# Another order of the steps of an attention and two-layer network kernel on one Trainium2 core

## The chip, the core and the metric

The kernel runs on one core of a Trainium2 chip. The metric is the time of one execution on the device in microseconds (us); shorter is better. A core has a matrix engine (TensorE, PE in the profile), a vector engine (VectorE, DVE), a scalar engine for functions like exp (ScalarE, ACT), a general engine (GpSimd, POOL), and SyncE (SP), which here issues DMA transfers. Each engine runs its own queue of instructions in order and waits at an instruction until what it needs is there. Operands lie in SBUF (the large on-chip memory); TensorE writes its sums to PSUM, a small memory of banks from which the other engines read them.

## The reference

Two stages. The first is attention with root-mean-square normalised q and k, for 8 batches and 12 heads of 448 rows of 64 values; the second takes the heads of a row as 768 features, multiplies by `w_in` (768 x 2048), applies a leaky rectifier with a slope per feature, and multiplies by `w_out` (2048 x 768).

```python
rms = np.sqrt(np.mean(x * x, axis=-1, keepdims=True) + 1e-06)   # for q and for k
q_n, k_n = q / rms_q * g_q, k / rms_k * g_k
scores = 1.0 / np.sqrt(64) * np.matmul(q_n, k_n.transpose(0, 1, 3, 2))
attn = np.exp(scores - np.max(scores, axis=-1, keepdims=True))
attn = attn / (np.sum(attn, axis=-1, keepdims=True) + 1e-09)
x = np.matmul(attn, v)                      # to 3584 rows of 768
h = x @ w_in
g = np.maximum(h, 0.0) + alpha * np.minimum(h, 0.0)
out = g @ w_out                             # 3584 x 768, float32
```

## The kernel before

**Steps.** The kernel is a set of small functions, one for each kind of step, and a string `PLAN` (lines 24 to 195) with 1324 calls of them. At its end a loop goes through `PLAN.split()` and calls one function for each word. The order of the words is the order in which every engine gets its instructions. Nothing reorders them afterwards; waits between engines follow from the data, and from the buffers that are used again. So the string is the schedule, written out by hand or by a program that made it.

**Attention.** The work is cut into 24 units y (three to a batch, four heads each) and seven slices j of 64 queries. For each unit:
- `load_qk(y)` (SP) brings q and k into tiles called `nat`, of which there are four, so q and k of two units (units 2, 5 and 8 use a lent piece of SBUF, `arena`). From unit 9 on it is `load_twice`, eight transfers on SP (L326). `load_v(b)` (GpSimd's queue, L334) brings v of a batch; there is one buffer for it, so the load waits for the attend steps of the batch before.
- `square` (GpSimd; L370 from unit 9 on, L381 before), `reduce` (VectorE, L391 or L400) and `root` (ScalarE, L421 and L422) make the norms; `scale` multiplies by them (GpSimd, L428 from unit 9 on, L441 before; for the first units VectorE). `fold`, `weigh`, and `turn` (TensorE transposes, L565) or `flip` (VectorE, L536) bring q and k into the layout for the products. Unit 0 does this in pieces, `part_square`, `part_reduce`, `part_root`, `part_scale` (L479), `part_turn`, `part_copy`.
- `score(y,j)` (TensorE, L593), `soft(y,j)` (ScalarE's exp, L607), `den` and `attend` (TensorE, L618 and L642: sums of the exponentials and their product with v), `log`/`invert` (ScalarE), and `times` (VectorE, L714), which writes `xT`.

**The two layers.** For each batch b, `up(b,ft)` (TensorE, L731, six matmuls; the first four of batch 0 start with `begin`) multiplies by a block of 128 of the 2048 columns, `slope` (ScalarE, L771) and `larger` (VectorE, L777) make the rectifier and write `gT`. Row tiles 0 to 5 go through `down` (TensorE, L797, 16 matmuls), `down_end` (VectorE, L808) and a send (SP, L783). Tiles 6 to 27 go in pairs by a scheme that saves matmuls in return for sums: `mix_weights` (GpSimd, L827) sums blocks of `w_out` once; for each pair, `mix_two(tile, engine)` and `mix_rest(tile)` sum blocks of `gT`, and the products are `qa1`, `qa2`, `qa3`, `qb1`, `qb2`, `qc1`, `qc2` (TensorE, L859) with steps `...v` of VectorE that add them up and send them. The last three pairs use `quad`.

The sums of a pair are these; `eng` is VectorE for the pairs 6 to 20 (`vec`) and GpSimd for the others (`pool`), and `mix_rest` is GpSimd's and reads `s2`:

```python
        eng.tensor_add(out=s1, in0=block(tile + 1, 0), in1=block(tile + 1, 1))   # L847
        eng.tensor_sub(out=s2, in0=s1, in1=block(tile, 0))                       # L848
```

**Buffers.** PSUM is split into three pools: two double banks for scores (`pss`), one double bank for den and attend (`psa`) and two single banks for the rest (`psf`). Steps take the buffers of a pool in turn. The last argument of score, up, den, attend, down, begin and the products, `spare`, sends a step to another pool than its own. Results on their way out lie in five buffers (`osb`, from `result()`); one is free again when its send is through. The weights are loaded in pieces on GpSimd's queue, `load_w_in(c)` (four or eight issues, L344 and L352) and `load_w_out(c)` (L358). `spin` is a matmul without a use, which keeps TensorE at work in the opening; `follow` is a small copy that holds GpSimd's queue to a place.

Of the kernel before, what the change touches and what calls it, by code (L numbers as in the profile page):

```python
# [24 lines left out]
opening() part_square(q,0:1,0:7,act) part_square(q,1:2,0:7,act) part_reduce(q,0:1,0:7)  # L25
part_reduce(q,1:2,0:7) part_root(q,0:7) load_v(0) load_w_in(1) part_square(k,0:2,0:3,act)
# [3 lines left out]
part_copy(q,0:7,vec) part_turn(k,r3-7) part_copy(k,0:3,vec) square(2,q) reduce(1,k) follow(0,k)  # L30
part_copy(k,3:7,vec) score(0,0,0) square(2,k) reduce(2,q,0) soft(0,0) score(0,1,0) root(1) spin(1)
scale(1,q) score(0,2,1) load_w_in(0) soft(0,2) square(3,q) scale(1,k) score(0,4,0) soft(0,1)
square(3,k) reduce(2,q,1) follow(1,k) score(0,3,1) turn_one(1,q) soft(0,4) score(0,6,0)
turn_one(1,k) reduce(2,k) spin(1) score(1,0,1) soft(0,3) score(1,2,0) soft(0,6) soft(1,0)
spin(2,0) spin(1) score(1,1,1) score(0,5,0) soft(1,2) root(2) spin(1) soft(1,1) score(1,6,0)
scale(2,q) soft(0,5) score(1,3,1) scale(2,k) load_w_in(2) reduce(3,q,None) load_qk(4) soft(1,3)
score(1,5,0) turn(2) score(1,4,1) soft(1,5) score(2,0,0) soft(1,6) soft(1,4) soft(2,0)
score(2,1,0) reduce(3,k,0+1) den(0+1,0) soft(2,1) attend(0+1,1,0) root(3) scale(3,q) log(0+1)
load_qk(5) score(2,3,1) score(2,4,0) invert(0+1) soft(2,4) attend(0+1,0,1) soft(2,3) score(2,2,0)
times(0+1,1,0) times(0+1,1,1) square(4,q) load_qk(6) spin(1,0) times(0+1,0,0) score(2,5,1)  # L40
scale(3,k) turn(3) reduce(4,q,None) load_w_in(3) load_qk(7) square(4,k) soft(2,2) score(2,6,0)
soft(2,5) soft(2,6) den(2,1) attend(2,0,1) score(3,0,1) score(3,1,0) square(5,q) log(2)
reduce(4,k,None) invert(2) root(4) begin(0) begin(1) times(2,0,0) up(0,0,0) begin(2) square(5,k)
up(0,1,0) begin(3) soft(3,0) slope(0,0) reduce(5,q) up(0,2,0) load_w_out(0) slope(0,1) larger(0,0)
reduce(5,k) square(6,k) up(0,3,1) up(0,4,0) soft(3,1) score(3,6,0) score(3,2,0) slope(0,4)
soft(3,2) larger(0,1) up(0,5,0) slope(0,2) up(0,6,0) scale(4,q) root(5) slope(0,3) soft(3,6)
square(6,q) larger(0,3) scale(4,k) score(3,3,0) larger(0,4) larger(0,2) load_w_out(1) scale(5,q)
square(7,q) reduce(6,q) load_v(1) slope(0,5) larger(0,5) follow(2,k) slope(0,6) score(3,5,0)
soft(3,5) turn(4) up(0,8,0) score(3,4,1) score(4,0,0) soft(3,3) score(4,4,0) up(0,9,0) slope(0,8)
scale(5,k) soft(4,0) up(0,11,0) larger(0,6) up(0,7,1) larger(0,8) up(0,10,0) load_w_out(2)  # L50
up(0,12,0) score(4,2,1) soft(3,4) slope(0,9) reduce(6,k) slope(0,11) score(4,3,0) larger(0,9)
slope(0,7) score(4,1,0) soft(4,4) up(0,13,0) slope(0,10) larger(0,11) load_qk(8) larger(0,7)
larger(0,10) slope(0,12) soft(4,2) larger(0,12) soft(4,1) slope(0,13) turn(5) up(0,14,0)
larger(0,13) soft(4,3) score(5,0,1) square(8,k) score(5,2,0) square(8,q) root(6) slope(0,14)
reduce(7,q) up(0,15,0) score(4,5,0) soft(5,0) larger(0,14) scale(6,k) soft(4,5) score(4,6,1)
slope(0,15) larger(0,15) down(0,0,0) reduce(8,q) score(5,6,0) scale(6,q) soft(5,2) score(5,1,0)
score(5,4,1) reduce(8,k) soft(4,6) soft(5,6) down(1,0,0) turn(6) score(5,3,0) load_w_out(3)
soft(5,4) den(3+4,1) square(7,k) attend(3+4,0,0) soft(5,1) reduce(7,k) soft(5,3) down_end(0,0)
log(3+4) mix_weights(0,1) invert(3+4) down_end(1,0) load_qk(9) score(5,5,0) score(6,0,0)
attend(3+4,1,0) root(7) down(2,0,1) scale(7,q) soft(5,5) soft(6,0) times(3+4,0,0) den(5,1)  # L60
mix_weights(0,0) times(3+4,1,1) attend(5,0,1) score(6,3,0) mix_weights(0,2) root(8) load_qk(10)
score(6,1,1) log(5) invert(5) down_end(2,0) times(3+4,1,0) down(0,1,0) times(5,0,2) scale(7,k)
times(5,0,3) score(6,4,1) score(6,5,0) scale(8,k) score(6,2,0) soft(6,1) times(5,0,0) times(5,0,1)
soft(6,3) down_end(0,1) turn(7) square(9,q) mix_weights(0,3) up(1,2,1) square(9,k) soft(6,4)
slope(1,2) up(1,1,0) soft(6,2) reduce(9,q) down(1,1,0) scale(8,q) up(1,0,0) larger(1,2)
score(7,0,0) score(6,6,0) up(1,4,1) slope(1,1) up(1,3,0) larger(1,1) score(7,4,0) down_end(1,1)
soft(6,5) slope(1,0) larger(1,0) score(7,3,0) soft(6,6) soft(7,0) slope(1,4) up(1,7,0)
mix_weights(1,0) reduce(9,k) slope(1,3) square(10,q) soft(7,3) slope(1,7) larger(1,4) up(1,5,1)
larger(1,3) larger(1,7) soft(7,4) turn(8) score(7,5,0) slope(1,5) soft(7,5) score(7,1,0) soft(7,1)
up(1,6,0) slope(1,6) load_v(2) larger(1,5) up(1,10,0) score(7,2,0) root(9) slope(1,10)  # L70
score(8,3,0) score(7,6,1) load_qk(11) square(10,k) up(1,9,0) up(1,8,0) reduce(10,q) larger(1,6)
scale(9,q) larger(1,10) soft(7,6) soft(7,2) up(1,13,1) up(1,11,0) slope(1,9) slope(1,8)
slope(1,13) reduce(10,k) slope(1,11) larger(1,9) larger(1,8) fold(10) scale(9,k) mix_weights(3,0)
root(10) larger(1,13) larger(1,11) up(1,12,0) scale(10,q) mix_weights(1,2) slope(1,12)
square(11,q) den(6+7,0) flip(9,k) score(8,0,0) scale(10,k) log(6+7) soft(8,0) up(1,15,0)
slope(1,15) up(1,14,1) load_qk(12) soft(8,3) down(2,1,0) larger(1,12) square(11,k) slope(1,14)
square(12,q) flip(9,q) score(8,1,0) larger(1,14) score(8,2,1) larger(1,15) score(8,4,0)
invert(6+7) down(3,0,0) down_end(2,1) soft(8,2) score(8,6,0) soft(8,1) score(8,5,1) soft(8,4)
down_end(3,0) weigh(9) soft(8,5) soft(8,6) reduce(11,q) flip(10,k) attend(6+7,0,1) times(6+7,0,0)
attend(6+7,1,0) times(6+7,1,0) flip(10,q) score(9,0,0) down(3,1,1) weigh(10) reduce(11,k) fold(11)  # L80
score(9,2,0) score(9,1,0) down_end(3,1) times(6+7,1,1) down(4,0,0) soft(9,0) root(11) soft(9,2)
# [1021 lines left out]
```

## Time and profile before

| what | value |
|---|---|
| time, median of 3 executions | 426.65 us (425.70 to 428.54) |
| the profiled execution, its own time | 428.47 us |
| its span in the profile | 426.4 us |
| TensorE's mean granted clock | 0.979 of full speed |

The profile is of one execution. Its span runs from the first to the last instruction that is seen; the time holds some 2 us more around it. A line such as L847 is a line of the kernel above. A row of a group has the line, engine, operation, the tile written and the tiles read with their shape and type, the number of instructions, then the busy time, the mean length in ns of one, and the engine's idle time just before them with who ended it. A row of a timeline has the start, the length, engine, line, operation and tiles, the number of instructions run together, and in brackets the idle time before and who ended it. A row of a window has the time from and to, its length, the busy time and count of PE, PE's weight loads, DVE, ACT and POOL, the granted clock, the busy share of the DMA engines (as an average of 16; the records let it pass 1) and GB/s. "issue" is idle time in which the engine waited for nothing that the profile shows.

### The profile page before, as it was taken

Reading aid. Unit: us, or ns where it says so; the run is one execution under the profiler, and the core shown is the slowest. Engines: PE = TensorE matmul, PEld = TensorE weight load, DVE = VectorE, ACT = ScalarE, POOL = GpSimd, SP = SyncE. Lnnn points to the kernel's source line nnn. Section 1 sums busy time; section 2 is a strip of 40 time slices with the busy share of each in tenths; the row PEclk is TensorE's granted clock in tenths of the full one; section 3 lists DMA queues with packets and bytes.
Section 4 is the critical chain, followed back from the end, with each engine's and each line's share of the span. In section 5 each row is a group of like instructions: output and inputs, shape, how many; then the busy total and the mean of one; then the engine's idle time right before and its main releaser. Section 6 shows DMA issues by size and latency. Waiting matters only on the chain. (4 is left out here: it accounts for less than half of the span.)

```text
span 426.4 us, 11986 instructions
## 1 busy us (share of the span) xinstructions
PE 402.5 (94%) x5083; PEld 211.3 (50%) x5083; DVE 289.3 (68%) x495; ACT 269.6 (63%) x405; POOL 269.3 (63%) x184
## 2 busy tenths in 40 slices
PE   7689999799999999999998999969989999999996
PEld 3334444355455545454455445534545445555564
DVE  3868865456837878697787968996798565464422
ACT  5488686437876686666875896857666875225210
POOL 7899867975585988975475866385464234700780
PEclk9599999799999999999999999999999999999999
DMA  8999795997393875763975965792602600320133
GB/s 240 248 230 238 137 243 95 195 231 143 83 223 97 213 165 97 177 159 97 208 160 120 204 155 133 149 237 83 156 20 49 111 2 22 73 59 0 29 93 102
DMA packets 37221, 58.39 MB, mean 137 GB/s; under 512 B 4768, under 2 KB 28976, under 8 KB 37168
## 3 DMA queue, kind: packets, MB, share of 16 engines
q1 hardware_dynamic: 23232, 45.43, 43.0%
q0 software_dynamic: 13536, 11.81, 18.5%
q8 instruction: 39, 0.64, 0.6%
q10 hardware_dynamic: 400, 0.39, 0.3%
q14 instruction: 14, 0.11, 0.1%
HBM read 58.40 MB, written 11.01 MB: 163 GB/s over the span
## 5 line engine op out<-in xcount | busy, mean ns | idle before, releaser
L607 ACT ACTIVATE expT<-sc 128x896 f16<-128x896 f32 x168 | 147.5, 916 | 58.6 <-PE sc L593 54.1
L731 PE MATMUL hT<-xT,w_in_sb 128*128 128x448 f16 x558 | 116.4, 353 | 4.5 <-DVE gT L777 3.9
L731 PEld LDWEIGHTS <-w_in_sb 128*128 128x128 f16 x768 | 72.5, 98 | 79.0 <-issue 15.6
L428 POOL TENSOR_TENSOR qs<-nat,rr 128x896 f16<-128x896 f32 x30 | 65.3, 2231 | 46.9 <-ACT rr L422 46.9
L777 DVE TENSOR_TENSOR gT<-hT,gT 128x448 f16<-128x448 f32 x93 | 57.5, 621 | 35.4 <-ACT gT L771 34.8
L771 ACT ACTIVATE gT<-hT,cols 128x448 f16<-128x448 f32 x92 | 58.2, 635 | 35.1 <-PE hT L731 34.5
L370 POOL TENSOR_TENSOR nat<-nat 128x896 f32<-128x896 f32 x30 | 50.9, 1700 | 15.3 <-DMA nat<-in_q_dram 9.4
L593 PE MATMUL sc<-qT,kT 64*32 64x448 f16 (+1 forms) x1092 | 51.0, 360 | 5.4 <-ACT expT L607 1.9
L859 PEld LDWEIGHTS <-gT 128*128 128x128 f16 x352 | 33.9, 98 | 24.3 <-issue 2.1
L731 PE MATMUL hTa<-xT,w_in_sb 128*128 128x448 f16 x198 | 42.9, 353 | 0.0
L593 PEld LDWEIGHTS <-kT 64*32 64x32 f16 (+1 forms) x1092 | 16.3, 94 | 34.9 <-issue 25.9
L391 DVE TENSOR_REDUCE sp<-nat 128x28 f32<-128x896 f32 x30 | 32.1, 1076 | 0.1
L714 DVE TENSOR_TENSOR xT<-av,rden 64x448 f16<-64x448 f32 (+1 forms) x37 | 27.2, 735 | 6.6 <-ACT rden L676 4.6
L777 DVE TENSOR_TENSOR gT<-hTa,gT 128x448 f16<-128x448 f32 x33 | 20.4, 619 | 13.8 <-ACT gT L771 13.6
L771 ACT ACTIVATE gT<-hTa,cols 128x448 f16<-128x448 f32 x33 | 21.0, 636 | 11.0 <-PE hTa L731 10.9
L618 PEld LDWEIGHTS <-vt 64*32 64x32 f16 x1344 | 20.3, 93 | 14.8 <-issue 5.0
L797 PEld LDWEIGHTS <-gT 128*128 128x128 f16 x192 | 18.9, 102 | 16.1 <-issue 5.5
L797 PE MATMUL op<-w_out_sb,gT 128*128 128x384 f16 x144 | 24.8, 326 | 0.0
L618 PE MATMUL av<-expT,vt 64*32 64x448 f16 x896 | 24.4, 349 | 0.0
L855 POOL TENSOR_TENSOR gT<-gT 128x1024 f16<-128x1024 f16 x11 | 23.9, 2172 | 0.6 <-DVE arena L847 0.6
L847 POOL TENSOR_TENSOR gs<-gT 128x1024 f16<-128x1024 f16 x3 | 6.4, 2117 | 26.8 <-DVE gT L777 26.8
L859 PE MATMUL qx<-w_out_sb,gT 128*128 128x384 f16 x112 | 19.7, 326 | 0.0
(154 smaller groups left out, 570.0 us busy)
## 6 DMA issues: line engine op xcount, KB each, us to landing
nat<-in_q_dram SPq DMA_DIRECT2D x60, 216.0 KB, 4.6
nat<-in_k_dram SPq DMA_DIRECT2D x60, 216.0 KB, 5.9
out_dram<-osb SPq DMA_DIRECT2D x107, 96.0 KB, 3.0
vt<-in_v_dram POOLq DMA_DIRECT2D x8, 672.0 KB, 7.4
w_in_sb<-in_moe_w_in_dram POOLq DMA_DIRECT2D x24, 128.0 KB, 8.1
w_out_sb<-in_moe_w_out_dram POOLq DMA_DIRECT2D x4, 768.0 KB, 8.5
nat<-in_k_dram SPq DMA_DIRECT2D x6, 448.0 KB, 7.8
nat<-in_q_dram SPq DMA_DIRECT2D x5, 448.0 KB, 7.2
```

What stands on the lines that cost most here:

```text
L370: nc.gpsimd.tensor_mul(out=sqs[y, nm], in0=t[:, :, :HD], in1=t[:, :, :HD])
L391: nc.vector.tensor_reduce(out=parts[y][:, ts("qk".index(nm), 4 * J), :1], in_=sqs[y, nm], axis=AXIS_X, op=ALU.add,)
L428: nc.gpsimd.tensor_mul(out=t.rearrange("p j d n -> p n j d"), in0=nat[y, nm][:, :, :HD].rearrange("p (n j) d -> p n j d", j=J), in1=r.unsq ...
L593: nc.tensor.matmul(out=sc[ds(64 * g + m * c, m), par, :S].rearrange("p (j c) -> p j c", j=J), lhsT=kT[ds(64 * par, 64), j, g, ts(c, m)], r ...
L607: nc.scalar.activation(out=expT[y][:, j], in_=scs[y, j][:, :, :S], func=AF.Exp, scale=QK_SCALE, bias=EXP_BIAS,)
L618: nc.tensor.matmul(out=accs[g][ds(32 * n, 32), :S], lhsT=weights(g, y, par, c, j), rhs=expT[y][ds(64 * g, 64), j, par, :], start=(j == 0), ...
L714: nc.vector.tensor_mul(out=o, in0=p, in1=q)
L731: nc.tensor.matmul(out=hT[:, :S], lhsT=w_in_sb[:, block_of(g, i), ts(ft, 128)], rhs=xT[b][:, g, i, :], start=(i == 0 and g == 0), stop=(i ...
L771: nc.scalar.activation(out=g, in_=hT[:, :S], func=AF.Copy, scale=alpha_sb[:, ft : ft + 1])
L777: nc.vector.tensor_max(out=g, in0=hT[:, :S], in1=g)
L797: nc.tensor.matmul(out=op[:, :OH], lhsT=gT[:, ft, ts(tile % J, 128)], rhs=w_out_sb[:, ft, ts(oh, OH)], start=(ft == 0), stop=(ft == NF - 1),)
L859: nc.tensor.matmul(out=bank[:, c], lhsT=g[:, ft], rhs=v[:, ft, c], start=(first and ft == 0), stop=(ft == HF - 1), skip_group_check=True,)
```

## The change

Only the string `PLAN` is another one: 1324 steps before and after, of each kind as many, so each engine has the same instructions with the same shapes. What differs is the order of the words and the last argument (`spare`, the PSUM pool) of some hundred steps. The table is one line shorter, so lines behind it have numbers lower by one in the kernel after. No function is touched.

The diff takes out nearly all of the table's lines and puts in others. These are the places that the prediction speaks of. The opening, before and after:

```diff
-opening() part_square(q,0:1,0:7,act) part_square(q,1:2,0:7,act) part_reduce(q,0:1,0:7)
...
-load_qk(3) part_square(k,0:2,3:7,act) part_reduce(k,0:2,0:3) part_reduce(k,0:2,3:7)
-part_root(k,0:3) part_scale(q,0:7,7,pool) part_scale(k,0:3,3,vec) part_turn(q,r0-7) square(1,q)
-reduce(1,q) part_root(k,3:7) part_scale(k,3:7,4,vec) part_turn(k,r0-3) gains() square(1,k)
...
-part_copy(k,3:7,vec) score(0,0,0) square(2,k) reduce(2,q,0) soft(0,0) score(0,1,0) root(1) spin(1)
-scale(1,q) score(0,2,1) load_w_in(0) soft(0,2) square(3,q) scale(1,k) score(0,4,0) soft(0,1)
+opening() part_square(q,1:2,0:7,act) load_w_in(1) part_square(q,0:1,0:7,act)
+part_reduce(q,0:1,0:7) part_reduce(q,1:2,0:7) part_root(q,0:7) part_square(k,0:2,0:3,act)
+part_reduce(k,0:2,0:3) part_square(k,0:2,3:7,act) part_reduce(k,0:2,3:7) part_root(k,0:3)
+square(1,q) part_scale(k,0:3,3,vec) load_v(0) reduce(1,q) spin(2,0) part_turn(k,r0-3)
+part_scale(q,0:7,7,pool) load_qk(3) part_turn(q,r0-7) gains() part_copy(q,0:7,vec)
+part_copy(k,0:3,vec) part_root(k,3:7) square(1,k) score(0,0,0) reduce(1,k) part_scale(k,3:7,4,vec)
+soft(0,0) square(2,q) score(0,1,1) reduce(2,q,0) part_turn(k,r3-7) part_copy(k,3:7,vec)
+score(0,2,1) spin(1) root(1) load_w_in(0) scale(1,k) scale(1,q) soft(0,1) score(0,3,0)
+score(0,5,0) soft(0,3) turn_one(1,k) turn_one(1,q) square(2,k) spin(1,0) score(0,4,0) reduce(2,k)
...
+soft(1,6) load_w_in(2) scale(2,q) scale(2,k) spin(1) soft(1,3) root(3) turn(2) soft(1,5)
+scale(3,q) soft(0,6) score(1,4,0) soft(1,4) score(2,0,0) score(2,1,1) scale(3,k) soft(2,0)
```

Units 13 to 15 and the sends of the first tiles:

```diff
-square(12,k) down(5,1,0) times(8,0,0) load_qk(13) times(8,0,1) mix_weights(1,1) down(4,1,0)
...
-slope(2,5) up(2,9,1) larger(2,3) reduce(13,q) larger(2,4) slope(2,8) load_qk(14) soft(10,4)
...
-qa2v(6) scale(13,q) load_qk(15) score(11,4,0) slope(2,15) score(11,1,0) reduce(14,q) reduce(14,k)
...
-score(12,0,0) score(11,2,0) scale(13,k) down_end(5,0) mix_two(6,vec) times(9+10,0,0) root(14)
+score(8,2,1) load_qk(12) score(8,3,0) down_end(2,1) weigh(9) load_qk(13) soft(8,1) down(3,0,0)
+score(8,5,0) soft(8,2) score(8,4,1) attend(6+7,0,1) square(11,q) score(9,0,0) down_end(3,0)
...
+scale(10,k) square(11,k) score(9,1,0) reduce(11,k) soft(8,5) load_qk(14) fold(11) mix_weights(1,2)
+times(6+7,1,0) soft(8,4) down_end(3,1) down(4,0,0) square(12,q) soft(9,0) times(6+7,1,1)
+flip(10,k) down_end(4,0) soft(8,6) load_qk(15) mix_weights(3,3) soft(9,1) root(11) score(9,5,0)
...
+larger(2,15) score(12,3,0) mix_weights(2,2) soft(12,0) scale(13,k) larger(2,13) mix_two(6,vec)
+qa3(6,0) mix_rest(6) down_end(5,0) times(9+10,0,0) qb1(6,0) mix_weights(3,0) times(9+10,1,0)
```

The sums of the pairs 12, 14 and 16:

```diff
-up(4,3,1) scale(17,k) up(4,4,0) soft(15,6) mix_two(12,vec) up(4,0,0) score(16,1,0) soft(16,3)
...
-larger(4,14) score(18,1,0) load_qk(22) root(20) qb2v(12) load_v(6) den_pre(17) attend(17,0,1)
-score(18,5,0) soft(18,1) log_pre(17) flip(19,k) scale(20,k) invert(17) flip(19,q) times(17,0,1)
...
-up(5,1,0) up(5,3,1) up(5,2,0) soft(18,2) slope(5,0) up(5,5,0) mix_two(14,vec) up(5,7,1) up(5,4,0)
-score(19,6,0) slope(5,1) square(21,q) score(19,1,0) soft(19,0) up(5,8,0) larger(5,0) slope(5,3)
-larger(5,1) up(5,6,1) scale(20,q) square(21,k) qa1(14,0) slope(5,2) qa2(14,0) score(19,4,0)
...
-attend(18+19,0,1) root(22) mix_two(16,vec) score(20,4,1) times(18+19,0,0) attend(18+19,1,0)
+mix_two(12,vec) score(16,3,1) load_v(5) soft(16,3) soft(15,1) up(4,1,0) up(4,4,0) slope(4,1)
...
+soft(18,1) qb2v(12) den_pre(17) load_qk(22) scale(19,k) log_pre(17) attend(17,0,1) flip(19,k)
+scale(20,k) invert(17) score(18,3,0) flip(19,q) times(17,0,0) score(18,5,1) qc2(12,0)
+score(18,2,1) square(21,q) qc1(12,0) soft(18,5) times(17,0,1) qc2v(12) times(17,0,3) scale(20,q)
+soft(18,2) square(21,k) times(17,0,2) weigh(19) square(22,q) qc1v(12) up(5,0,0) score(19,1,0)
+score(18,4,1) score(19,0,0) up(5,1,0) soft(18,3) up(5,5,1) reduce(21,q) slope(5,0) mix_two(14,vec)
...
+slope(5,7) slope(5,8) load_v(6) slope(5,4) larger(5,2) up(5,6,1) soft(19,0) soft(19,1) larger(5,7)
...
+score(20,5,0) log(18+19) larger(5,15) flip(21,q) mix_two(16,vec) attend(18+19,0,1) score(20,1,1)
```

More of the change, by code (lines that the diff above doesn't have):

```diff
@@ L37 @@
[L37 to L48, printed above, removed]
@@ L55 @@
[L55 to L66, printed above, removed]
@@ new lines @@
+times(9+10,1,1) soft(12,3) fold(14) score(11,2,1) score(11,6,0) qa3v(6) qb1v(6) score(11,5,0)
+qb2(6,0) qc2(6,1) flip(13,k) soft(11,3) square(15,q) soft(11,2) root(14) qc1(6,0) qb2v(6) qc2v(6)
+qc1v(6) score(12,2,1) load_qk(16) scale(14,q) flip(13,q) score(12,1,0) reduce(15,q) soft(11,6)
+soft(11,5) weigh(13) score(12,6,0) den_pre(11) attend(11,0,0) soft(12,2) soft(12,1) mix_two(8,vec)
+soft(12,6) log_pre(11) score(13,0,0) score(13,3,0) invert(11) qa1(8,0) square(15,k) times(11,0,3)
+soft(13,0) qa1v(8) qa2(8,0) qa3(8,0) times(11,0,1) qb1(8,0) score(13,1,0) soft(13,3) qa2v(8)
@@ new lines @@
+slope(3,14) larger(3,14) square(17,k) score(14,6,0) soft(14,5) qa1(10,0) reduce(17,q) qc2(8,0)
+qa2(10,1) score(14,4,0) attend(12+13,0,1) reduce(17,k) soft(14,6) fold(17) soft(14,3) log(12+13)
+weigh(15) scale(16,q) invert(12+13) mix_two(10,vec) qa1v(10) attend(12+13,1,0) root(17) qc2v(8)
+soft(14,4) qa2v(10) score(15,0,0) times(12+13,0,0) times(12+13,1,0) soft(15,0) score(15,2,0)
+qa3(10,1) score(15,3,0) times(12+13,1,1) flip(16,k) flip(16,q) soft(15,2) weigh(16) den_pre(14)
+attend(14,0,1) score(15,4,0) soft(15,3) score(16,0,1) qa3v(10) mix_rest(10) load_qk(19)
```

260 lines of the change are left out of this document (131 added, 129 removed).

## The prediction

> **What bounds the kernel now.** The page comes first: its span and the busy time of each engine.
>
> ```profile
> span 426.4 us, 11986 instructions
> ...
> PE 402.5 (94%) x5083; PEld 211.3 (50%) x5083; DVE 289.3 (68%) x495; ACT 269.6 (63%) x405; POOL 269.3 (63%) x184
> ...
> L428 POOL TENSOR_TENSOR qs<-nat,rr 128x896 f16<-128x896 f32 x30 | 65.3, 2231 | 46.9 <-ACT rr L422 46.9
> ...
> L370 POOL TENSOR_TENSOR nat<-nat 128x896 f32<-128x896 f32 x30 | 50.9, 1700 | 15.3 <-DMA nat<-in_q_dram 9.4
> ```
>
> TensorE (PE) is busy for 402.5 of 426.4 us, and the other engines for about two thirds. The change alters no instruction, only the order and the pools of PSUM (the accumulator memory), so TensorE's work stays. It can win at most 426.4 − 402.5 = 23.9 us of TensorE idle, plus what a low TensorE clock costs; it can lose without a bound. The last two rows price one GpSimd scale (2.23 us) and one square (1.70 us). Next, the view of waits, for TensorE alone (sum, count, longest):
>
> ```profile
> PE hT L731 <- DVE gT L777: 3.9, 2, 3.2
> PE avb L618 <- issue: 2.7, 1, 2.7
> ...
> PE sc L593 <- ACT expT L607: 1.9, 3, 0.8
> ...
> PE sc L593 <- DVE xT L714: 1.4, 1, 1.4
> ...
> PE tps L565 <- POOL qs L441: 0.6, 2, 0.3
> ```
>
> Three waits, 3.9 in two pieces and 1.4, go to VectorE although VectorE has slack on average. The 2.7 is a pause for which no engine is to blame. Much of the rest stands before 41.3 us, in the opening. I take these three places in turn.
>
> **VectorE's sums.** The view of lines, shapes kept apart, has VectorE's additions and subtractions of two f16 SBUF operands (`mix_two(…,vec)`, one L847 and one L848 each):
>
> ```profile
> L847 DVE TENSOR_TENSOR arena<-gT 128x1024 f16<-128x1024 f16 x7 | 10.8, 1542 | 0.0
> L848 DVE TENSOR_TENSOR arena<-arena,gT 128x1024 f16<-128x1024 f16 x7 | 7.9, 1135 | 0.2
> L847 DVE TENSOR_TENSOR gs<-gT 128x1024 f16<-128x1024 f16 x1 | 0.7, 682 | 0.0
> L848 DVE TENSOR_TENSOR gs<-gs,gT 128x1024 f16<-128x1024 f16 x1 | 0.7, 694 | 0.0
> ```
>
> The same size takes 0.68 and 0.69 us in one unit and 1.54 and 1.14 us on the mean of seven. So the excess is 10.8 + 7.9 − 7 × (0.68 + 0.69) = 9.1 us of VectorE's time. The timeline shows where the largest piece comes from:
>
> ```profile
> 273.79 0.88 POOL L334 DMA_DIRECT2D vt<-in_v_dram  x1 [7.21 <-PE av L618]
> ...
> 276.72 1.71 POOL L370 TENSOR_TENSOR nat<-nat 128x896 f32<-128x896 f32 x1
> 278.36 2.23 POOL L428 TENSOR_TENSOR qs<-nat,rr 128x896 f16<-128x896 f32 x1
> 280.38 1.72 POOL L370 TENSOR_TENSOR nat<-nat 128x896 f32<-128x896 f32 x1
> 283.46 2.12 POOL L855 TENSOR_TENSOR s<-gT,arena 128x1024 f16<-128x1024 f16 x1 [1.36 <-DVE arena L848]
> ```
> ```profile
> 277.64 5.01 DVE L847 TENSOR_TENSOR arena<-gT 128x1024 f16<-128x1024 f16 x1
> 282.69 0.69 DVE L848 TENSOR_TENSOR arena<-arena,gT 128x1024 f16<-128x1024 f16 x1
> ```
> ```profile
> 283.97 1.29 PE L731 MATMUL hT<-xT,w_in_sb 128*128 128x448 f16 x6 [3.22 <-DVE gT L777]
> ```
>
> `load_v(6)` held GpSimd 7.21 us for an attend step; then its late work ran back to back, until 280.38 + 1.72 = 282.10. VectorE's sum began at 277.64 and ended at 282.65, 0.55 after GpSimd ran dry; the next one, beside an idle GpSimd, took 0.69. Behind it stood the step that frees a PSUM bank, and TensorE waited 3.22. Of the excess of 5.01 − 0.68 = 4.33 us, 1.1 was covered. Two more sums reached TensorE:
>
> ```profile
> 237.57 2.13 DVE L847 TENSOR_TENSOR arena<-gT 128x1024 f16<-128x1024 f16 x1
> ```
> ```profile
> 313.17 4.67 POOL L428 TENSOR_TENSOR qs<-nat,rr 128x896 f16<-128x896 f32 x2 [4.13 <-ACT rr L422]
> 313.35 2.43 DVE L848 TENSOR_TENSOR arena<-arena,gT 128x1024 f16<-128x1024 f16 x1
> ```
>
> These are `mix_two(12)`, with 3.9 − 3.22 = 0.66 of TensorE's waits, and `mix_two(16)`, with 1.37 (the 1.4 above). All the sums together cost TensorE 0.66 + 3.22 + 1.37 = 5.25 us.
>
> The new table puts each of VectorE's sums ahead of a GpSimd step that must wait for it (`mix_rest`) or for TensorE (`load_v`). I laid it out by the durations of the rows above. (6), (8), (10), (18) and (20) meet a GpSimd that has nothing to run; none cost TensorE anything before, so this gives 0. (12) is clean: −0.66. (16) stands in a long pause, but its neighbours `times` and `attend` come closer: −1.37 + 0.25, my estimate from that layout (0 to 0.7). (14) is not clean. Behind `root(20)` GpSimd has scale(20,k), square(21,q), scale(20,q), square(21,k), square(22,q), and only then `load_v(6)`, which the change moves behind them. VectorE reaches the sum about 0.5 us into square(21,k): there are 2 × 1.70 − 0.5 = 2.9 us to wait, less the cover of 1.1, so about 1.8 at `up(5,3)`. Bounds: 0 if GpSimd is 3 us earlier, 3.22 as now. I take 1.8, by the row at 277.64, where the sum waited until GpSimd was dry. The moved `load_v(6)` has its attend behind it by then, holds nobody, and its data are needed only by `attend(18+19)`, after all of up(5). Sum of this part: −0.66 − 3.22 + 1.8 − 1.37 + 0.25 = **−3.2**.
>
> The Trainium skill, page "SBUF — State Buffer", section "Who interferes with whom", says that a VectorE instruction with two SBUF inputs contends with a GpSimd instruction that reads SBUF, and that whoever issues first holds the shared ports for the whole instruction. That GpSimd blocks the sum, the trace bears out; that the sum waits for one instruction it does not, since 5.01 us cross the ends of two (278.43 and 280.59). By the page the sum at (14) would wait for square(21,k) alone, 1.2 us, nearly all under cover; that is rival C.
>
> **The opening.** Rows from the timelines of ScalarE, VectorE, GpSimd and TensorE:
>
> ```profile
> 14.96 0.92 ACT L607 ACTIVATE expT<-sc 128x896 f16<-128x896 f32 x1 [4.32 <-PE sc L593]
> ```
> ```profile
> 11.34 1.43 DVE L479 TENSOR_TENSOR qs<-nat,rr 128x512 f16<-128x512 f32 x1
> ```
> ```profile
> 17.15 2.20 POOL L344 DMA_DIRECT2D w_in_sb<-in_moe_w_in_dram  x4
> ...
> 22.35 3.47 POOL L381 TENSOR_TENSOR nat<-nat 128x896 f32<-128x896 f32 x3
> ```
> ```profile
> 27.30 1.09 PE L565 MATMUL tps<-ident,qs 128*128 128x128 f16 x14
> ...
> 36.57 0.96 PE L565 MATMUL tps<-ident,arena 128*128 128x128 f16 x14
> ...
> 41.30 0.93 PE L731 MATMUL hT<-xT,w_in_sb 128*128 128x448 f16 x4
> ```
>
> The second half of k's part_scale (1.43) moves behind what the first score needs, so the first exponential comes at about 14.3 instead of 14.96. Against that, `load_w_in(0)`, eight DMA issues between 17.15 and 22.35, now stands ahead of `square(2,k)` on GpSimd, where before it stood behind; the square ends some 5 us later. `load_qk(3)` on SP's queue is issued about 3 us later, and `reduce(3,k)` precedes scale(2) on VectorE. So turn(2), at 27.30, comes between 28.4 and 29.8. turn(3), at 36.57, comes earlier, at about 33, as scale(3,q) no longer waits behind copies. What matters is when `begin(0)`, the first matmul of the second half of the work, starts (41.30): between 40.7 and 43.3, by the longer or the shorter of the two chains. TensorE's steps ahead of it are the same, so the shift goes straight to the end: I take **+0.8**, from −0.6 to +2.
>
> **What the rest of the order does.** Score(12,1) no longer waits for its softmax (0.8, the longest of three in the row above) and `qa3(6)` waits 0.3 for its bank instead: **−0.5**. turn(4) and turn(6) no longer wait for GpSimd's scale (the 0.6): **−0.5**. New short waits stand where banks of PSUM change pool: turn(8) beside up(1,6), the end of up(3), up(4,4). I find about 0.2 to 0.3 at each, **+0.6**, bounded by 0 and by 1.5 (two of 0.8, the longest of such waits now). In the last 50 us, where up(7) and the last groups run, I find no idle in either order: 0.
>
> On SP's queue the loads `load_qk(13)`, `(14)` and `(15)` move ahead of the sends of down_end(3,0) to (5,1) and qa2v(6); a load waits until GpSimd's scale of two units before has read its buffer, and all sends behind it wait too.
>
> ```profile
> SPq L326 <- POOL qs L428: 73.5, 21, 11.2
> ```
>
> SP already waits 73.5 us in this way. There are five output buffers. By my layout the buffer that `qb1v(6)` needs is back 1.5 us before TensorE must wait for it, and `attend(9+10,1)` has 1.0 us over the sum `mix_two(6)` that stands ahead of its bank's release. So I take 0, and this is rival E.
>
> **The sum.** 0.8 − 3.2 − 0.5 − 0.5 + 0.6 = −2.8. The profiled execution took 428.47 us by its own count (span 426.4 and 2.1 around it), 1.8 above the median of 426.65. So the profile would come to about 425.7 and the median to **423.8**. With the bounds of the unknown terms, this case reaches from 421 to 427.
>
> **The pause for which no engine is to blame.**
>
> ```profile
> 81.53 1.32 PE L618 MATMUL avb<-expT,vt 64*32 64x448 f16 x23 [2.70 <-issue]
> 82.78 5.03 PE L797 MATMUL opa<-w_out_sb,gT 128*128 128x384 f16 x16
> ...
> 90.36 2.77 PE L797 MATMUL op<-w_out_sb,gT 128*128 128x384 f16 x16
> ```
> ```profile
> 82.00:88.00 6.00, 6.00 (x63) 2.57 (x55) 0.78 (x2) 1.26 (x3) 4.88 (x4) 0.55 1.03 242
> 280.00:290.00 10.00, 6.78 (x49) 3.18 (x48) 9.81 (x12) 4.86 (x8) 6.31 (x4) 1.00 0.93 220
> ```
> ```profile
> q8 instruction: 39, 0.64, 0.6%
> ```
>
> In the middle of an attend TensorE stopped for 2.70 us, with the DMA engines full (share 1.03 in the window behind it, 242 GB/s); then the clock was 0.55 and a down step took 5.03 instead of 2.77. Together 2.70 + 2.26 = 5.0 us. After the 3.22 at 283.97 the clock stayed at 1.00. I read the pause as a late fetch of instructions behind data. The number of instructions is unchanged, and the last weights are in flight here in the new order too, with load_w_out(3) issued earlier relative to the attend. I leave it in.
>
> The Trainium skill, page "Runtime: NRT & Kernel Launch", section "Instruction fetch mechanics", says that instructions come in blocks by a DMA queue of the engine's own and that the cost is mostly hidden. The trace shows the queue (39 packets) and one place where something was not hidden.
>
> **The rivals.**
> - **B, the pause goes.** The weights land earlier or the block falls elsewhere: −5.0 on the forecast, 418.8. For it: there is a single such pause in 426 us. Against it: the same transfers crowd the same stretch. 0.17.
> - **C, the sums are all clean and the opening loses nothing.** −1.8 − 0.8: 421.2. For it: in the new order GpSimd never stands behind load_v(6). 0.15.
> - **D, the change doesn't do what it says.** GpSimd is late everywhere, its pauses are no pauses, and the sums cost their 5.25 again: 423.8 + 3.2 = 427.0. 0.07.
> - **E, slower: SP's queue and the output buffers.** If GpSimd, between 100 and 180 us, is late by a scale and a square (3.93), the load of unit 15 holds the sends as long, TensorE loses 3.93 − 1.0 = 2.9, and the gain is gone: 426.7. Late by two such pairs it loses 6.9, and if the clock then falls as at 82.78, another 2.3: 430.7 to 433. It decides from 1 us of lateness on, and loses more than the kernel of before from 3.8 on. For it: SP waits for just these scales 21 times now, up to 11.2 us. Against it: the layout by the old durations leaves slack. 0.28.
>
> **How the numbers follow.** The forecast has 0.33. A change of 1%, 4.3 us, is about what a measurement of this kernel can tell from none. Below 422.4 lie B, most of C and a tenth of the forecast: 0.35. Above 430.9 lies most of E and little else: 0.23. The rest is 0.42. The range goes from 416.5 (B, with most of C) to 432 (E without its far end).
>
> **What would show it.** In the changed profile: the eight sums of L847 at about 0.68 to 0.7, with one exception of 3 to 4 us near 280; TensorE's waits for gT and xT down from 5.25 to about 2; begin(0) within a microsecond of 42; TensorE still waiting 2.7 for issue near 80, with a low clock after it. I am wrong in the mechanism if the sums stay at 1.5 on the mean, and in the cover if the sums are short but waits for buffers of L783's sends or for mix steps appear between 100 and 180 us.

## The result

The kernel after takes 422.14 us (median of four executions, 420.98 to 422.88), against 427.2 us before (four executions on the same chip, 425.7 to 428.54). The ratio is 0.988, with a 95% interval of 0.9838 to 0.9922: 5.06 us or 1.2% faster. The forecast was 423.8, 2.85 under the 426.65 that stood then as the median of before (three executions). On another chip, side by side with the last three experiments, the two stood at 421.51 and 428.06, a ratio of 0.9851 (0.9825 to 0.9877). Of all executions told of here, two ran at a lower clock and longer than the others of their kernel, 432.13 us of the run with moved loads and 429.43 of before beside it, and the ratios leave them out.

The profiled execution took 422.27 us. Its page answers to the first lines shown of before:

```profile
span 420.5 us, 11981 instructions
...
PE 400.3 (95%) x5083; PEld 211.9 (50%) x5083; DVE 281.8 (67%) x495; ACT 270.0 (64%) x405; POOL 268.4 (64%) x184
```

The span is 5.9 us shorter. TensorE's idle time fell from 426.4 − 402.5 = 23.9 to 420.5 − 400.3 = 20.2, and its busy time, for the same instructions, by 2.2. So two thirds of the gain are waits. The mean clock is nearly the same (0.979 before, 0.980 now), so it is other work that falls into the slow stretches: the down step at 82.78, 5.03 before, takes 2.77 here. The view of TensorE's waits (sum, count, longest) has other rows than before:

```profile
PE sc L592 <- DVE kT L499: 3.7, 1, 3.7
PE dnb L641 <- issue: 2.7, 1, 2.7
PE sc L592 <- ACT expT L606: 2.5, 3, 1.4
...
PE dn L617 <- issue: 1.1, 1, 1.1
...
PE qx L858 <- DVE xT L713: 0.2, 1, 0.2
```

The two rows that VectorE's sums had caused, 3.9 and 1.4, are gone; the last row, 0.2, comes behind `mix_two(16)`, whose sums took 0.65 and 0.69, and waits for a `times` step of VectorE. The pause of 2.7 "issue" is no longer at attend(3+4,1) but at den_pre(14), where 1.3 stood before. And the first row is new: the first score waits 3.7 for VectorE. In the view of lines by shape, VectorE's sums are all short:

```profile
L847 DVE TENSOR_TENSOR arena<-arena,gT 128x1024 f16<-128x1024 f16 x7 | 4.8, 691 | 0.2
L846 DVE TENSOR_TENSOR arena<-gT 128x1024 f16<-128x1024 f16 x7 | 4.7, 677 | 0.0
```

Their means fell from 1542 and 1135 ns to 677 and 691, which is what one takes beside an idle GpSimd. The forecast had left one of them long, `mix_two(14)`. The timelines of GpSimd and VectorE at that place:

```profile
273.82 2.21 POOL L427 TENSOR_TENSOR qs<-nat,rr 128x896 f16<-128x896 f32 x1
275.84 1.69 POOL L369 TENSOR_TENSOR nat<-nat 128x896 f32<-128x896 f32 x1
281.29 1.68 POOL L369 TENSOR_TENSOR nat<-nat 128x896 f32<-128x896 f32 x1 [3.76 <-DMA nat<-in_q_dram]
```
```profile
277.87 0.68 DVE L846 TENSOR_TENSOR arena<-gT 128x1024 f16<-128x1024 f16 x1
```

square(21,k) ended at 277.53, and square(22,q), which the forecast had put right behind it, waited 3.76 us for its load. The sum ran in that hole. VectorE also reached it later than forecast: 2.03 us after the start of square(21,k), where the layout had 0.5.

The opening shows the same kind of clash with another victim. Timelines of GpSimd and VectorE:

```profile
9.46 1.70 POOL L478 TENSOR_TENSOR qs<-nat,rr 128x896 f16<-128x896 f32 x1
11.11 1.68 POOL L380 TENSOR_TENSOR nat<-nat 128x896 f32<-128x896 f32 x1
12.74 1.81 POOL L380 TENSOR_TENSOR arena<-arena 128x448 f32<-128x448 f32 x2
```
```profile
10.58 4.00 DVE L1034 TENSOR_TENSOR gain<-cols 128x1 f32<-128x1 f32 x1
```

`gains()` multiplies two columns of 128 values. It took 0.16 us before and 4.00 here, from 10.58 to 14.58, just until GpSimd's run of four instructions ended at 14.55. The first score came at 15.49 instead of 14.32, and begin(0), the start of the second half, at 46.12 instead of 41.30:

```profile
46.12 1.12 PE L730 MATMUL hT<-xT,w_in_sb 128*128 128x448 f16 x5
```

### The profile page after: what moved, and what is told of

Its sections match the earlier page's. It is cut to its first block, busy times and chain, and to the rows that moved or that the text cites. A ratio compares the mean times of both kernels' runs of the same rounds, so it can differ in the third digit from the quotient of the medians.

```text
span 420.5 us, 11981 instructions
## 1 busy us (share of the span) xinstructions
PE 400.3 (95%) x5083; PEld 211.9 (50%) x5083; DVE 281.8 (67%) x495; ACT 270.0 (64%) x405; POOL 268.4 (64%) x184
## 4 chain that ended last, share of the span: by engine, by line
PE 91%; DVE 3%; DMA 1%; issue 1%; ACT 1%; POOL 1%; POOLq 0%; DVEq 0%
PE hT L730 24%; PE hTa L730 10%; PE sc L592 9%; PE op L796 6%; PE av L617 5%; PE qx L858 5%; PE qz L858 4%; PE qc L858 4%; PE oq L858 3%; PE avb L617 3%; PE dn L617 3%; PE qxa L858 3%; PE oqm L858 2%; PE qca L858 2%; DMA arena<-in_g_k_dram 1%; PE spin L1004 1%
## 5 line engine op out<-in xcount | busy, mean ns | idle before, releaser
L730 PE MATMUL hT<-xT,w_in_sb 128*128 128x448 f16 x540 | 112.4, 353 | 0.1
L770 ACT ACTIVATE gT<-hT,cols 128x448 f16<-128x448 f32 x89 | 56.3, 634 | 36.5 <-PE hT L730 35.9
L776 DVE TENSOR_TENSOR gT<-hT,gT 128x448 f16<-128x448 f32 x90 | 55.7, 620 | 35.7 <-ACT gT L770 35.2
L730 PE MATMUL hTa<-xT,w_in_sb 128*128 128x448 f16 x216 | 46.8, 353 | 0.0
L858 PEld LDWEIGHTS <-gT 128*128 128x128 f16 x352 | 33.5, 98 | 25.3 <-issue 3.7
L713 DVE TENSOR_TENSOR xT<-av,rden 64x448 f16<-64x448 f32 (+1 forms) x37 | 27.2, 735 | 12.9 <-ACT rden L675 7.8
L770 ACT ACTIVATE gT<-hTa,cols 128x448 f16<-128x448 f32 x36 | 22.9, 635 | 15.2 <-PE hTa L730 14.9
L776 DVE TENSOR_TENSOR gT<-hTa,gT 128x448 f16<-128x448 f32 x36 | 22.3, 620 | 12.6 <-ACT gT L770 12.4
L796 PE MATMUL op<-w_out_sb,gT 128*128 128x384 f16 x160 | 27.5, 326 | 0.1
L617 PE MATMUL av<-expT,vt 64*32 64x448 f16 x896 | 25.5, 360 | 0.0
L796 PEld LDWEIGHTS <-gT 128*128 128x128 f16 x192 | 18.3, 98 | 14.2 <-issue 2.3
L854 POOL TENSOR_TENSOR gT<-gT 128x1024 f16<-128x1024 f16 x11 | 23.9, 2172 | 0.6 <-DVE arena L846 0.6
L854 POOL TENSOR_TENSOR gs<-gT,gs 128x1024 f16<-128x1024 f16 x4 | 8.5, 2123 | 21.7 <-DVE gs L847 21.5
```

The source lines that it names most:

```text
L617: nc.tensor.matmul(out=accs[g][ds(32 * n, 32), :S], lhsT=weights(g, y, par, c, j), rhs=expT[y][ds(64 * g, 64), j, par, :], start=(j == 0), ...
L730: nc.tensor.matmul(out=hT[:, :S], lhsT=w_in_sb[:, block_of(g, i), ts(ft, 128)], rhs=xT[b][:, g, i, :], start=(i == 0 and g == 0), stop=(i ...
L770: nc.scalar.activation(out=g, in_=hT[:, :S], func=AF.Copy, scale=alpha_sb[:, ft : ft + 1])
L776: nc.vector.tensor_max(out=g, in0=hT[:, :S], in1=g)
L796: nc.tensor.matmul(out=op[:, :OH], lhsT=gT[:, ft, ts(tile % J, 128)], rhs=w_out_sb[:, ft, ts(oh, OH)], start=(ft == 0), stop=(ft == NF - 1),)
L854: nc.gpsimd.tensor_sub(out=o, in0=a, in1=b)
```

## The experiments

A block shows the words of the table that move, with "..." where others lie between.

**Is it the multiplication of the gains that makes the opening late?** Two runs. The first lets the multiplication read one operand from PSUM; the second also puts `load_w_in(0)` back behind `square(2,k)`.

```diff
-            out=gain, in0=cols[:, NF : NF + 1], in1=cols[:, NF + 1 : NF + 2]
+            out=gain, in0=held_ct[0][:, NF : NF + 1], in1=cols[:, NF + 1 : NF + 2]
```
```diff
 score(0,2,1) spin(1) root(1)
-load_w_in(0)
 ...
 turn_one(1,q) square(2,k)
+load_w_in(0)
```

> The changed kernel with one edit: the 128x1 multiplication of the gains reads one operand from PSUM instead of a copy in SBUF. Theory A (the multiplication, 4.00 us in the changed kernel and 0.16 before, waited until GpSimd ran dry at 14.51, and this is where the opening lost its time): it takes about 0.2 us, the first score starts near 11.8 instead of 15.49, begin(0) comes 3 to 4.8 us earlier (41.3 to 43 instead of 46.12), and the time falls by 3 to 4 to about 418.5. Theory B (the opening is set by GpSimd's chain load_w_in(0), square(2,k), turn(2)): the multiplication is short, the first score early, but begin(0) stays within 1 us of 46.1 and the time within 1 us of the changed kernel's.

> As the run before, and load_w_in(0) moved behind square(2,k) on GpSimd, where the old order had it. Theory A: begin(0) within 0.7 us of the run before, since VectorE's delay was the cause. Theory B: only now begin(0) comes to about 42, 4 us earlier than in the run before, and the time falls by as much.

The first took 421.41 us (419.19 to 423.42), the second 422.34 (420.43 to 423.71), beside 426.97 before. The multiplication took 0.16 in both. But begin(0) came at 46.14 and 46.35, and the first score at 15.43 and 15.48, as in the changed kernel. In the first run's timeline of VectorE another operation had become the long one:

```profile
8.96 3.20 DVE L478 TENSOR_TENSOR qs<-nat,rr 128x384 f16<-128x384 f32 x1
...
13.27 0.16 DVE L1034 TENSOR_TENSOR gain<-ct,cols 128x1 f32<-128x1 f32 x1
```

That is the first part of k's `part_scale`, 0.55 in the changed kernel. It started after GpSimd's run had begun, at 8.40 in this execution, and was held instead. So the clash is real, and which operation it hits turns on when the loads land. Theory A of these runs fell in its second half: the clash does not set begin(0). The second execution of the changed kernel shows it best.

> The changed kernel once more, to stand beside the next three on one chip: 420 to 423. If VectorE's small operations in the opening are held or free by chance, the place of the long one (gains 4.00 in the first profile) differs: another operation with two SBUF operands is long, or none, and begin(0) lies between 44 and 46.5.

It took 421.51. Here nothing was held: the multiplication took 0.16, the first part of `part_scale` 0.76, and the first score started at 12.47, three us earlier than in the first profile. The rows of its TensorE that follow:

```profile
29.98 1.79 PE L564 MATMUL tps<-ident,qs 128*128 128x128 f16 x14
36.24 0.96 PE L564 MATMUL tps<-ident,arena 128*128 128x128 f16 x14 [1.11 <-DVE arena L440]
45.91 1.31 PE L730 MATMUL hT<-xT,w_in_sb 128*128 128x448 f16 x6
```

begin(0) still came at 45.91. In its chain of waits, the load of v holds `load_w_in(0)` on GpSimd until 22.20, square(2,k) stands behind that, and turn(2) behind both; then scale(3,q) on VectorE takes 3.78 beside GpSimd, where 1.09 is usual, and turn(3) waits for it. Theory B has this chain right, yet the run that put square(2,k) ahead of the loads did not start earlier either. There the first score was late again, and turn(2) followed it by 16.2 us; with the old opening it follows by 12.4 to 13.5, in eight executions.

Two more things differ in that stretch. Between the first score and turn(2), TensorE's scores waited 2.1 to 3.5 us for a softmax in all six profiles with the new opening, and 0.8 to 1.1 in all eight with the old one. And TensorE's clock fell a second time. The window of 28 to 32 us in the two profiles of the changed kernel, then in two runs from below with the same opening (`v6_early`, `qk18_late`); behind from, to and length stand PE, PE's weight loads, VectorE, ScalarE, GpSimd, clock, DMA share and GB/s:

```profile
28.00:32.00 4.00, 4.00 (x19) 1.39 (x12) 2.09 (x2) 3.67 (x7) 3.98 (x7) 0.61 0.90 127
28.00:32.00 4.00, 4.00 (x24) 2.08 (x20) 3.44 (x6) 2.62 (x5) 3.89 (x10) 0.50 0.52 62
```
```profile
28.00:32.00 4.00, 2.40 (x43) 1.36 (x50) 3.87 (x5) 3.11 (x5) 3.98 (x9) 1.00 0.77 107
28.00:32.00 4.00, 3.39 (x57) 1.84 (x64) 3.23 (x5) 3.88 (x7) 3.98 (x7) 1.00 0.99 159
```

The four profiles with a clock of 0.50 to 0.63 there have begin(0) at 45.9 to 46.4, the two with 1.00 at 44.4 and 43.6. So about 2 us of the lateness come together with the low clock, and 2 to 3 stay without it, against 41.3 before. The old opening has this second fall too, in two of its eight profiles, with begin(0) at 42.1 and 43.7. No run changed the clock by itself.

**What do VectorE's sums cost, and what holds them?** One run undoes the move of `load_v(6)` in the changed kernel; the other makes it alone in the kernel before.

```diff
 attend(17,0,1) flip(19,k)
+load_v(6)
 scale(20,k) invert(17)
 ...
 slope(5,7) slope(5,8)
-load_v(6)
```

> The changed kernel with load_v(6) back ahead of scale(20,k) on GpSimd, as the old order had it; nothing else. Theory A (a sum of VectorE waits until GpSimd runs dry): GpSimd is held until attend(17) and then runs five steps back to back; mix_two(14)'s first sum takes 4 to 5 us instead of 0.68, TensorE waits 2.5 to 3.5 in up(5), and the time rises by about 3 to 425. Theory B (it waits only for the one instruction that runs when it starts): the sum takes at most 2.3, TensorE waits under 0.7, and the time rises by under 1.

It took 424.62 us (423.84 to 427.29, ten executions), 0.9963 of before (0.9934 to 0.9991), where the changed kernel had 0.988. The timelines of GpSimd, VectorE and TensorE:

```profile
271.35 0.88 POOL L333 DMA_DIRECT2D vt<-in_v_dram  x1 [8.53 <-PE av L617]
...
275.90 2.23 POOL L427 TENSOR_TENSOR qs<-nat,rr 128x896 f16<-128x896 f32 x1
277.93 1.71 POOL L369 TENSOR_TENSOR nat<-nat 128x896 f32<-128x896 f32 x1
```
```profile
277.01 3.18 DVE L846 TENSOR_TENSOR arena<-gT 128x1024 f16<-128x1024 f16 x1
```
```profile
281.50 1.67 PE L730 MATMUL hT<-xT,w_in_sb 128*128 128x448 f16 x8 [2.79 <-DVE gT L776]
```

The sum started 1.12 us before the end of the scale that was running, and finished 0.55 after the end of the square behind it, when GpSimd had nothing left. So here too it waited for the run, not for the one instruction. At 3.18 it is shorter than the 4 to 5 expected, because square(22,q) had to wait for its load here too; TensorE's wait of 2.79 is within what theory A said, and so is the time.

```diff
 qb2v(12)
-load_v(6)
 den_pre(17) attend(17,0,1)
 ...
 scale(20,q) square(21,k)
+load_v(6)
```

> The kernel of before with load_v(6) moved behind square(21,k) on GpSimd; nothing else. If this load set the 3.22 us wait: mix_two(14)'s first sum takes 0.7 instead of 5.01, TensorE's wait of 3.22 in up(5) is gone and the time falls by about 3 to 424. If the order around it is tight anyway, a wait for another step of up(5) or of the pair 14 takes its place and less than 1 us is won.

> The old order with load_v(6) moved alone, once more. Theory A (the move takes away the 3.2 us wait and no more; the 6.4 of the first run were in part chance): 3 to 4 below the kernel before, 1 to 2.5 above the changed kernel. Theory B (it is worth as much as the whole change): within 1 of the changed kernel.

One word moved in the old table gave 420.55 (419.83 to 422.74) beside 426.97, and on the second chip 423.11 (421.2 to 425.66) beside 428.06, a ratio of 0.9896 (0.9863 to 0.9929), there 1.6 above the changed kernel. In both profiles the first sum took 0.68 and the second 2.05, and of the 3.22 only 0.25 was left. The first run's 6.4 is more than the wait that went. Part of it may be chance: the pause at attend(3+4,1) happened to be 1.4 in its profile, and 2.6 in the second's:

```profile
PE avb L618 <- issue: 1.4, 1, 1.4
```
```profile
PE avb L618 <- issue: 2.6, 1, 2.6
```

The second run lies 1.6 above the changed kernel, as theory A had it, but won 4.95 where 3 to 4 was expected. The wait can cost more than its length: in the second profile of before, told of next, the clock fell behind it and the up steps that followed took 3.99 instead of 2.43.

**Do the pauses for instructions belong to the order?** First the kernel before once more.

> The kernel of before, profiled once more. If the 2.70 us pause at attend(3+4,1) and the low clock behind it belong to the old order, they stand here again, within half a us; if they come and go from execution to execution, the pause is under 1.5 or the clock behind it is full, and the gain there in the changed kernel's profile is no gain of the order. mix_two(14) must take about 5 us and cost TensorE about 3.2 in either case.

427.0 us, and the pause stands again; the clock behind it does not fall. The waits and one window (from, to, length, busy time of PE, PEld, DVE, ACT, POOL, clock, DMA share, GB/s):

```profile
PE hT L731 <- DVE gT L777: 3.9, 2, 3.2
PE avb L618 <- issue: 2.5, 1, 2.5
```
```profile
84.00:88.00 4.00, 4.00 (x130) 2.22 (x129) 1.89 (x4) 1.68 (x3) 3.18 (x3) 1.00 1.01 228
```

So the pause at attend(3+4,1) is the old order's (2.70, 2.47, 1.42 and 2.57 in its four profiles), and the 2.26 us of low clock behind it came in the first of them only. Then the changed kernel with the eight loads of unit 18 two sends later:

```diff
 qc1v(8)
-load_qk(18)
 ...
 qc2v(8) soft(14,4) qa2v(10)
+load_qk(18)
```

> The changed kernel with the eight loads of load_qk(18) moved behind the two sends of qa2v(10) on SP's queue. Theory A (TensorE's pause of 2.3 to 2.7 us at den_pre(14) is a block of instructions that comes late because the loads fill the DMA engines from 218 to 227): the block is fetched before the loads, the pause is under 0.7, the clock behind it stays at 1.00, and the time falls by 2.5 to 4. Theory B (the pause belongs to that place in the stream of instructions whatever is in flight): still 1.2 to 2.7 at den_pre(14), the time within 1 of the changed kernel, or above it as unit 18 comes later.

418.77 us (418.42 to 419.87, three executions), 0.9849 of before (0.9801 to 0.9897). The windows of the changed kernel and of this run, around den_pre(14):

```profile
220.00:224.00 4.00, 4.00 (x127) 2.19 (x104) 3.07 (x6) 2.37 (x4) 4.00 (x3) 1.00 1.03 227
...
226.00:230.00 4.00, 2.82 (x92) 2.64 (x99) 1.15 (x3) 0.58 (x2) 4.00 (x3) 0.61 0.93 225
```
```profile
216.00:220.00 4.00, 4.00 (x101) 2.29 (x106) 3.19 (x7) 3.54 (x6) 2.33 (x2) 1.00 0.08 21
...
226.00:230.00 4.00, 3.49 (x22) 1.85 (x19) 3.84 (x7) 1.35 (x2) 0.98 (x2) 1.00 1.05 230
```

By its ratio that is no faster than the changed kernel's two, 0.988 and 0.9851, so the time alone decides nothing; the rows do. In the changed kernel the DMA engines are full (1.03) when TensorE uses up its instructions fastest, 56 short matmuls and as many weight loads in an attend. The packet records have its blocks of 16,384 bytes: one at 212.03, the next only at 224.79, inside the pause. With the loads moved, the engines are nearly idle (0.08) at 216 to 220, a block comes at 218.97 and another at 223.94, den_pre(14) has no pause, and the clock stays at 1.00. The other runs agree: den_pre(14) waits 2.2 to 2.7 in all seven profiles of the changed order with the loads in their place, and not at all in the three with the loads moved. What took its place: 0.51 us for issue a little later, and a wait of 1.46 at up(4,4), as theory B's last clause had it. VectorE's rows show why:

```profile
234.85 1.08 DVE L390 TENSOR_REDUCE sp<-nat 128x28 f32<-128x896 f32 x1 [1.79 <-POOL nat L369]
235.86 0.61 DVE L776 TENSOR_TENSOR gT<-hT,gT 128x448 f16<-128x448 f32 x1
```

reduce(18,k) waits for the later load, and the step that frees TensorE's bank stands behind it on VectorE.

The Trainium skill, page "Runtime: NRT & Kernel Launch", section "Instruction fetch mechanics", has the 16 KiB blocks and a DMA queue of the engine's own. Their size agrees; that the cost is mostly hidden holds for all but two of the 40 blocks here; those two stand beside waits of 1.1 and 2.7 us.

**Does the late opening go through to the end?** The old table up to begin(0), then the changed one without what is done already (no short diff: the first 128 steps are the old table's, the last 1124 the changed one's).

> The old order up to begin(0), then the changed order with what is done already taken out. So far begin(0) came at 41.3 and 42.1 in the two profiles with the old opening, and at 44.4 to 46.4 in the four with the new one. Theory A (the new opening costs 2.5 to 5 us, and these go straight to the end): begin(0) at 41 to 42.5, and the time 2.5 to 4 below the changed kernel, 418 to 419.5. Theory B (what is late at begin(0) is caught up by later slack, as transfers and weights set the stretch to 90 us): begin(0) as early, but turn(7) not before 91 and the time within 1 of the changed kernel.

419.9 us (417.91 to 421.39), a ratio of 0.9878 to its own runs of before. begin(0) came at 42.52 and turn(7) at 87.92, against 46.12 and 92.05; the lead of 3.6 to 4.3 stood until up(7,0), 366.55 against 370.83. The profile, which is of the fastest of the six executions, bears out theory A. The time does not: the ratio equals the changed kernel's 0.988, where 2.5 to 4 us were expected. The two kernels were not on one chip, so what the lead is worth in the median stays open. With `load_qk(18)` moved as well:

> Both edits together. If both theories A hold, the gains add: 5 to 7.5 below the changed kernel, about 415 to 417. If only the opening counts, as the run hyb.

418.95 (416.6 to 421.37): the two gains did not add. In its profile a clash in the opening came back, on the second part of `part_scale`, and the wait at up(4,4) was 2.09:

```profile
10.53 4.16 DVE L478 TENSOR_TENSOR qs<-nat,rr 128x512 f16<-128x512 f32 x1
```

So the old opening is open to the same clash. The next run keeps GpSimd out of VectorE's way there.

```diff
-        if (y, nm) == (1, "q"):
+        if y == 1:
             nc.scalar.activation(out=sqf, in_=src, func=AF.Square)
```
```diff
 part_copy(k,0:3,vec)
+follow(0,k)
 square(2,q) reduce(1,k)
-follow(0,k)
```

(and the gains from PSUM, as above)

> The old opening with the changed order behind it, and GpSimd kept out of VectorE's way in the opening: square(1,k) on ScalarE, the gains multiplied from PSUM, and follow(0,k), which waits for k's part_scale, ahead of square(2,q) on GpSimd. Theory A (the lock there costs 0 to 3.5 us by chance): no operation of VectorE before 15 us takes over 1.2 us but the first part_scale of k, the first score starts by 13.2, begin(0) by 42, and the time is 1 to 2.5 below the run hyb's 419.9, with a smaller spread. Theory B (the loads' landings set the start anyway): begin(0) as in hyb, 42.5, and the time within 1.

419.26 us (418.44 to 422.61), 2.25 under the changed kernel on the same chip. No operation ahead of the first score took over 1.33, and that score started at 12.80; but begin(0) came at 43.65. turn(2) had waited 2.0 for a scale, and behind it TensorE ran at 0.50 from 28 to 32 us. Theory A fell at begin(0); how much of the lateness is the order and how much the clock, one profile does not tell. What keeping the clash out is worth stays open as well: the time is within 1 of the 419.9 of `hyb`, but on another chip, and the ratios to each chip's own runs of before are 0.9812 (0.9778 to 0.9845) here and 0.9878 there.

**The edits together.** The last run adds three moves: `load_qk(18)` as above, and

```diff
 square(18,k) qc2v(10)
-reduce(18,k)
 ...
 slope(4,1) up(4,3,1) larger(4,1)
+reduce(18,k)
```
```diff
-score(3,6,0)
 times(2,0,0) begin(0) begin(1)
+score(3,6,0)
```

> As the run before, with load_qk(18) behind qa2v(10)'s sends, reduce(18,k) behind larger(4,1) on VectorE, so that the later load holds up no bank of up(4), and score(3,6) behind begin(1). If the pause at den_pre(14) and VectorE's wait at up(4,4), 1.5 to 2.1 in the two runs with the late load, are what is left there: no pause over 0.7 between 215 and 245, no wait of the 1.4 us kind at score(3,6), and 3 to 5 below the run before, about 414. If a pause for instructions only goes elsewhere: another pause of 1 to 2.5 us, and at most 1.5 won.

414.86 us (413.57 to 416.89), 0.9699 of before (0.9668 to 0.973) and 6.65 under the changed kernel on that chip. Its page and the largest rows of TensorE's waits:

```profile
span 411.8 us, 11983 instructions
```
```profile
PE tps L489 <- DVE gain L1034: 1.7, 1, 1.7
PE spin L1004 <- DVE gT L266: 1.5, 1, 1.5
...
PE qz L858 <- issue: 0.5, 1, 0.5
```

No wait over 0.5 us is left behind 30 us, no pause stands at den_pre(14), and 4.4 was won on the run before, within the 3 to 5 expected. Since these two stood on one chip, this is also the time that the three moves are worth together; none of them was measured alone there.

## Why the prediction came out right, and where its steps were wrong

The time lay in the range and on the side forecast. The steps behind it did worse than their sum, and of the four signs that it named, begin(0) near 42 and the pause near 80 failed. Each step in the order of the prediction, in the profiled execution:

- **The sums, −3.2 forecast.** TensorE's waits for them went from 5.25 to 0.2: −5.05. The mechanism was right: a sum waits until GpSimd's run ends, as the run with the early `load_v(6)` showed once more. Wrong was the one term of +1.8 at (14), because the layout had square(22,q) ready when its data were 3.76 us away, and VectorE at the sum before square(21,k) ended, where it came 0.34 after. So all sums were clean as in rival C, but not for C's reason. The rule of the Trainium skill, page "SBUF — State Buffer", section "Who interferes with whom", had given next to no wait there because the holder is one instruction; the sum of 3.18 us, which went on past the end of the scale and through the square, speaks against that reading. That whoever issues first holds the other, a pair of scales in the run `hyb_open` bears out: VectorE's, first by 0.11, took its usual 1.09, and GpSimd's 2.53 where 1.70 is usual. Not every pair does: in `v6_early` VectorE's came 0.83 ahead of GpSimd's, while GpSimd was issuing transfers, and took 4.14.

```profile
32.04 1.09 DVE L440 TENSOR_TENSOR arena<-nat,rr 128x896 f16<-128x896 f32 x1 [1.77 <-ACT rr L421]
```
```profile
32.15 2.53 POOL L440 TENSOR_TENSOR arena<-nat,rr 128x896 f16<-128x896 f32 x1
```

- **The opening, +0.8 forecast with bounds of −0.6 and +2.** It cost +4.8 at begin(0), which came between 43.6 and 46.4 in six profiles with the new opening and between 40.5 and 42.1 in four of the old order; the four runs that join the old opening to the changed order have it at 40.8 to 44.0. This is the step that failed most. The forecast had turn(2) between 28.4 and 29.8 and turn(3) at about 33; they came at 31.69 and 36.44. TensorE's idle time ahead of begin(0) is 11.1 to 12.9 us in those six and 7.2 to 8.7 in the first four. Of the 4.8, 1.1 is a pause for "issue", at den(2,1). The prediction looked at the landings and the queues of SP and GpSimd and took the first score as the anchor. But the first score moved between 12.47 and 15.49 and begin(0) did not follow it. Which step of the new opening costs the 3 us between first score and turn(2) is not settled: the multiplication is out, and so are it and the place of load_w_in(0) together. What the rows show there is the scores' longer wait for the softmax (2.5 us against 1.1) and the second fall of the clock. One row of that stretch was not tried: of the idle-time matmuls (`spin`), a row of 1.86 us at low clock stands directly ahead of turn(2) in the new order.
- **Score(12,1), −0.5, and turn(4), turn(6), −0.5.** The wait of 0.8 at 176.20 is gone, and the short waits between begin(0) and 79 us, 0.6 of them a pause for "issue", fell from 1.5 to 0.2: −0.8 and −1.3.
- **New short waits, +0.6.** One of 0.2 us at score(4,6) and the 0.2 at qa3(16): the bound of 0 was nearer.
- **The pause, left in.** At attend(3+4,1) it went: −2.70, and −2.26 of clock that the old order has in some executions only. At den_pre(14) it grew from 1.28 to 2.70, and TensorE ran there at 0.61. The prediction took the pause for a thing of one place with weights in flight. The runs show it at several stretches of dense short matmuls with the DMA engines full, and at den_pre(14) it goes with the place of the loads; rival B had half of it.
- **SP's queue, 0, rival E.** No wait over 0.2 us stands between 80 and 220 us. GpSimd was busy without a break from 120 to 130 and from 140 to 150, so it was near, but its lateness reached nobody.

```profile
120.00:130.00 10.00, 10.00 (x178) 5.23 (x177) 5.91 (x11) 6.98 (x9) 10.00 (x7) 1.00 0.59 146
```

Added up: 4.8 − 5.05 − 5.0 + 1.4 + 1.1 − 0.8 − 1.3 = −4.85 of the span's −5.9, where 1.1 is attend(14)'s length of 2.57 less the usual 1.51. The other 1.0 is not assigned. So an opening 4.0 us dearer than forecast stood against sums 1.85, pauses 2.5 and short waits 1.7 cheaper, and that the forecast came out close is luck.

## What to carry to other kernels

When an operation of VectorE with two SBUF operands is long in some places and short in others, look at what GpSimd runs beside it, and look at every such operation, not only at the large ones: a product of 128 values held VectorE for 4 us here. A pause for "issue" in a stretch of many short matmuls went here with what filled the DMA engines in the eight us before it. So look at the loads there: one moved by two sends, with two companions, won 4.4 us, where the new order of everything had won 5 to 6.5. And in a table of steps, find the one word that carries the gain: moving a single load that held GpSimd's queue won most of what the whole new table won, and in the profiled execution the new table's opening cost nearly as much as its sums gained.

## What the runs showed of the hardware that was not expected

- An instruction of VectorE with two SBUF operands that GpSimd holds stays held over the boundary between two of GpSimd's, while these follow each other without a pause: 5.01 over two ends before, 3.18 over one in the run with the early load, 4.00 and 4.16 over three in the opening. It ends 0.03 to 0.6 us after the last of them.
- A pause of TensorE of 2.1 to 3.2 us is followed by a lower clock in some executions and not in others: 2.70 was at 81.53 (0.55) and 2.47 at the same place was not (1.00); 2.70 at 227.18 was (0.61); 3.22 at 283.97 was not (1.00), and 3.21 at the same place in the second profile of before was (0.72 over the window of 280 to 284). Behind begin(0), no pause of 1.52 us or less was, in any of the profiles.
- The same kernel's first score varied by 3 us between two executions (15.49 and 12.47) with the same time at the end.
